# Two hand-kept issue orders of a convolution-and-attention kernel laid anew: the second convolution and the second attention

## The chip, the cores and the metric

The kernel runs on one core of one Trainium2 chip. The time is device microseconds of one execution, and the median of three executions of the kernel before is 421.01 us (420.74 to 422.48). The core has five instruction streams that run on their own and meet at semaphores: TensorE (PE in the profile, with PEld its weight loads), VectorE (DVE), ScalarE (ACT), GpSimd (POOL) and SyncE (SP), which here only issues DMAs. An engine takes its instructions in the order in which the program emitted them; an instruction that waits holds up all that stand behind it on the same engine.

## The reference: what is computed

`x` is `A_u`, 2048 tokens of 512 channels in bf16. Four residual layers are applied, two kinds twice each:

```
x = x + A(layernorm(x))      # convolution, first
x = x + B(layernorm(x))      # attention, first
x = x + A(layernorm(x))      # convolution, second
x = x + B(layernorm(x))      # attention, second
```

`A` is a diagonal state-space layer: a kernel `K[d, l]`, the real part of a sum over 128 poles, is convolved with each channel over all 2048 tokens by FFT (causal, padded to 4096), and `u * Dskip` is added. `B` is a local attention with 32 heads of 16 channels: `qkv = x @ wqkv`; a token looks at 8 keys, itself and those 2, 4, ... 14 tokens back, keys before the first token are masked, softmax over the 8, and the result goes through `wo`.

## The kernel before

**Layout.** Token `16 p + j` lies in partition `p` at index `j` of the residual tile `X` (128 partitions, 16 values of `j`, 512 channels), which stays in the chip's memory from start to end. Channels are handled in four chunks `dc` of 128; `cp` names the half of the channels (chunks 0 and 1, or 2 and 3). In the attention `fp` is a half of the heads and `jh` a half of the `j`.

**How order is set.** Every layer records its steps with `Plan.op`, each with its engine letter and the steps that it needs, and `Plan.either` records several ways to do one step (on another engine, or by DMA). `Plan.run` then emits the steps in the order of a row of numbers, `ORDERS[turn]`: turn 0 is the convolution kernel and the first convolution, turn 1 the first attention, turn 2 the second convolution (`a_layer`), turn 3 the second attention (`b_layer`). A row of numbers so sets two things: the order on every engine, and which of the ways is taken, since only the numbers of that way are in the row. Nothing is planned at run time.

**The second convolution** (`a_layer`), for each chunk `dc`:

- `s1`: PE multiplies the normed `U` by `F1` (L1120), and ACT or DVE copies the sums to `Z` (L1124).
- `turn`: a quarter `c` of `Z` is turned, either by a transposing DMA that SP issues (L1135), or by PE (L1141) with a copy to `zt` by ACT or DVE (L1145).
- `s2`: PE (L1161), and ACT copies to `xc` (L1165).
- `load`: the spectrum of the kernel, tile `Kt`, comes from DRAM scratch. POOL or SP loads it whole in two DMAs of 256 KB (L1224), or SP loads half of it in two of 128 KB (L1229, "once") and DVE copies it to the other partitions (L1234, "other"). The ring holds 8 of these tiles, of 16 in all.
- `product`: DVE multiplies `xc` by `Kt` (L1174).
- `inverse`: PE (L1186), and ACT or DVE copies to `VT` (L1189), as a whole or in two halves.
- `final`: PE adds `X` (L1204, L1207), and ACT or DVE writes `X` (L1212).

**The second attention** (`b_layer`):

- `start`: `X` is turned into `XT` (printed as `U`) by SP's transposing DMAs (L1318) or once by PE (L1312, L1315). DVE gathers the row statistics of a token group, for 512 channels at once into `ln_st` (L200), or for 256 at a time into `pst` (L1370), which can begin when one half of the channels is there; then the aggregates (L204, L1374) and the root on ACT (L1385, L1386).
- `pairs`: the reciprocal deviations `rs` are moved down a partition by PE (L1412) with a copy (L1414), DVE forms the products `rr` (L1417), ACT spreads them to `RR` (L1397), and POOL sets a few entries to one (L1403).
- `pair` and `proj`: PE projects queries and keys (L1450, L1431), and copies follow (L1455, L1436); `ahead` copies the end of the keys to the front (L1473). `values` projects the values (L1485), copied with a scale to `VX` (L1496), and SP moves some of them down a partition (L1509).
- `logits`: DVE multiplies q by k (`prod`, L1530) and PE sums (`Lp`, L1541); a copy, a turn and a copy lay them out as `L` (L1559, L1567, L1572).
- `softmax`: POOL masks (L1617), DVE scales by `RR` (L1610), takes the maximum in three steps (L1591) and subtracts it (L1655, or PE does); ACT takes the exponential, PE sums (`ps_den`, L1647), ACT inverts (L1628, L1632), and DVE multiplies (L1675).
- `pv`: DVE multiplies values by weights (`prod`, L1706) and PE sums into `po`; ACT copies to `ot` (L1748), and SP turns it into `oT` (L1753).
- `out`: PE multiplies by `wo` (L1818), row group `j` by row group. There are four ways to add the residual: PE adds it by an identity matmul and ACT copies (way 0 in the lower row groups); DVE adds from PE's sums (L1793); ACT copies to `sp` (L1797) and DVE adds (L1800); or ACT copies and POOL issues an adding DMA (L1803).
- `stored`: SP or ACT issues the store of a row group (L1967).

```
self.ops.append((fn, flat(after), self.way))
...
order = [int(i) for i in ORDERS[Plan.turn].split()]
...
for i in order:
    fn, after, way = self.ops[i]
    assert done.issuperset(after)
    fn()
```

Of the kernel before, what the change touches and what calls it, by code (L numbers as in the profile page):

```python
# [231 lines left out]
def load_params(nc, pp, prm):  # L232
# [53 lines left out]
    "792 813 936 747 853 854 741 843 789 742 935 938 750 855 937 844 845 748 751 870 939 940 869 821 822 859 752 753 872 "  # L286
    "871 790 829 830 812 873 860 943 942 862 861 924 925 926 910 946 874 911 912 945 948 863 864 947 865 876 867 949 877 "
    "950 953 951",
    "388 127 32 47 4 165 52 128 134 135 141 160 143 146 151 147 6 272 152 155 11 12 170 18 20 23 24 179 184 177 178 358 "
    "28 30 359 68 365 366 192 193 372 373 379 381 194 195 66 67 227 56 228 205 206 197 57 95 216 217 58 96 230 37 198 "  # L290
    "204 248 249 412 413 106 107 407 408 255 256 262 269 270 219 73 264 208 231 74 436 76 399 232 220 394 109 84 437 85 "
    "221 42 209 386 77 215 78 98 110 111 414 87 415 241 242 99 100 439 383 88 92 447 282 448 93 425 426 238 239 120 384 "
    "417 284 121 387 418 419 289 315 316 304 305 117 428 429 299 283 118 337 338 392 393 450 307 294 326 327 275 451 452 "
    "430 308 318 440 441 278 319 320 340 341 329 330 347 310 467 331 458 311 351 352 469 460 348 349 464 465 461 462",
    "34 87 44 1 122 33 178 8 121 149 130 259 151 36 119 63 136 229 9 179 230 231 180 196 120 150 62 64 65 205 125 37 148 "
    "152 50 206 207 197 198 202 35 181 93 203 182 204 260 38 247 183 232 261 274 248 275 233 39 126 40 41 42 153 265 216 "
    "66 386 388 390 391 389 124 392 123 127 393 387 249 234 276 319 128 67 172 223 224 173 394 400 175 320 225 176 325 "
    "326 395 398 399 396 397 401 402 286 287 406 408 412 410 292 293 289 290 310 311 313 314 283 284 404 405 418 407 316 "
    "317 307 308 298 280 299 302 177 419 420 421 422 413 281 409 411 414 343 423 344 334 335 295 296 352 328 353 322 474 "
    "476 323 337 424 338 416 475 417 453 477 480 331 332 304 305 429 430 431 481 478 479 482 375 376 454 438 455 340 341 "  # L300
    "363 484 364 485 355 356 456 507 346 347 457 511 349 508 358 350 486 487 359 509 512 462 463 366 367 460 369 461 370 "
    "360 361 488 384 441 489 372 378 373 379 385 439 440 490 493 495 494 381 496 445 497 498 499 442 382 443 444 446 447 "
    "506 449 450 452 464 465 521 519 466 523 520 524 522 525 526 473 527 513 514 510 533 530 534 537 529 515 517 518 547 "
    "532 804 805 806 832 833 784 785 535 822 767 548 823 824 549 550 536 551 552 553 768 786 558 559 538 560 539 540 794 "
    "839 567 568 580 541 569 576 581 544 808 795 578 543 577 579 582 572 852 583 546 574 573 575 570 840 571 584 587 599 "
    "588 600 853 601 602 591 592 810 595 597 939 855 586 598 589 593 706 596 590 702 594 603 841 921 925 926 694 922 708 "
    "796 695 703 709 707 927 696 697 883 923 834 873 924 704 698 968 699 884 908 813 857 700 705 701 874 906 863 710 864 "
    "940 811 859 953 954 854 941 955 971 969 893 904 894 862 909 974",
]


# [1691 lines left out]
```

## Time and profile before

| what | value |
|---|---|
| median of 3 executions | 421.01 us |
| profiled execution, its own time | 421.17 us |
| span of the profiled execution | 419.4 us, 13672 instructions |
| DVE busy | 393.0 us, 94% |
| PE busy | 355.7 us, 85% |
| ACT busy | 326.4 us, 78% |
| POOL busy | 29.1 us, 7% |
| second convolution | from about 268 to 308 us of the span |
| second attention | from about 308 us to the end |

Busy time is the sum of an engine's instructions, and neighbours on DVE and ACT overlap by some hundredths of a microsecond, so a group's mean is a little more than what one more of its kind adds. The view by windows gives the busy time of each engine within a stretch and the granted PE clock; where an engine is busy for nearly the whole stretch, it sets the pace there. The timeline gives in brackets the idle time ahead of a group and the releaser. SP's DMA rows show the issue, and the landing comes later.

### The profile page before, as it was taken

Reading aid. Unit: us, or ns where it says so; the run is one execution under the profiler, and the core shown is the slowest. Engines: PE = TensorE matmul, PEld = TensorE weight load, DVE = VectorE, ACT = ScalarE, POOL = GpSimd, SP = SyncE. Lnnn points to the kernel's source line nnn. Section 1 sums busy time; section 2 is a strip of 40 time slices with the busy share of each in tenths; the row PEclk is TensorE's granted clock in tenths of the full one; section 3 lists DMA queues with packets and bytes.
Section 4 is the critical chain, followed back from the end, with each engine's and each line's share of the span. In section 5 each row is a group of like instructions: output and inputs, shape, how many; then the busy total and the mean of one; then the engine's idle time right before and its main releaser. Section 6 shows DMA issues by size and latency. Waiting matters only on the chain. (4 is left out here: it accounts for less than half of the span.)

```text
span 419.4 us, 13672 instructions
## 1 busy us (share of the span) xinstructions
PE 355.7 (85%) x5866; PEld 226.9 (54%) x5866; DVE 393.0 (94%) x652; ACT 326.4 (78%) x534; POOL 29.1 (7%) x99
## 2 busy tenths in 40 slices
PE   2268867987998989999975999899999999966995
PEld 1153645776786764446732444677874456632452
DVE  6999999999999887989999999999999999999994
ACT  7999999899999574678963599999966788762730
POOL 2000000000000200010100303020000010000331
PEclk9999999999999999999999899999999999995899
DMA  7997248697989666002336277899972000352496
GB/s 212 214 294 265 95 57 166 151 163 176 167 129 167 135 166 125 19 2 70 89 98 91 54 151 140 167 182 199 202 87 57 19 2 2 88 134 56 52 174 143
DMA packets 103538, 52.01 MB, mean 124 GB/s; under 512 B 82923, under 2 KB 95356, under 8 KB 103222
## 3 DMA queue, kind: packets, MB, share of 16 engines
q1 hardware_dynamic: 97638, 44.46, 51.6%
q0 software_dynamic: 3376, 5.37, 6.8%
q10 hardware_dynamic: 2464, 1.31, 1.1%
q8 instruction: 46, 0.75, 0.8%
q14 instruction: 14, 0.11, 0.1%
HBM read 19.30 MB, written 6.29 MB: 61 GB/s over the span
## 5 line engine op out<-in xcount | busy, mean ns | idle before, releaser
L1706 DVE TENSOR_TENSOR prod<-VX,L 128x512 bf16<-128x512 bf16 (+2 forms) x72 | 75.5, 1102 | 0.5 <-ACT VX L1496 0.2
L1530 DVE TENSOR_TENSOR prod<-qT,kT 128x4096 bf16<-128x4096 bf16 (+1 forms) x40 | 72.3, 1857 | 0.5 <-ACT kT L1436 0.3
L1818 PE MATMUL ps_o<-wo_t,oT 128*32 128x512 bf16 x512 | 33.9, 395 | 0.4 <-DMA oT<-ot 0.4
L1485 PE MATMUL ps_v<-wv,U 128*128 128x256 bf16 x256 | 31.6, 272 | 1.7 <-ACT VX L1496 1.0
L877 ACT CAST Z<-ps_s 128x1024 bf16<-128x1024 f32 (+1 forms) x36 | 31.9, 931 | 0.5 <-PE ps_s L874 0.4
L1431 PE MATMUL ps_qk<-U,wqk 128*128 128x512 bf16 x128 | 30.3, 380 | 0.7 <-ACT qT L1436 0.7
L1496 ACT ACTIVATE VX<-ps_v,rs 128x256 bf16<-128x256 f32 x64 | 26.8, 472 | 3.8 <-PE ps_v L1485 3.0
L1485 PEld LDWEIGHTS <-U 128*128 128x128 bf16 x256 | 24.5, 97 | 9.6 <-issue 5.1
L1450 PE MATMUL ps_qk<-U,wqk 128*128 128x512 bf16 x128 | 28.8, 379 | 0.8 <-ACT X L1212 0.8
L1541 PE MATMUL Lp<-prod,sb_bones 128*32 128x512 bf16 x256 | 22.3, 409 | 5.6 <-DVE prod L1530 5.6
L1748 ACT CAST ot<-po 128x1024 bf16<-128x1024 f32 (+1 forms) x15 | 14.4, 985 | 14.2 <-PE po L1721 10.5
L1721 PE MATMUL po<-prod,sb_ident 32*32 32x512 bf16 x768 | 17.1, 428 | 7.5 <-DVE prod L1706 7.3
L894 PE MATMUL xp<-zt,sb_C 128*128 128x512 bf16 x64 | 18.9, 379 | 4.2 <-ACT zt L914 2.3
L1818 PEld LDWEIGHTS <-oT 128*32 128x32 bf16 x512 | 13.1, 99 | 14.7 <-issue 3.5
L1431 PEld LDWEIGHTS <-wqk 128*128 128x128 bf16 x128 | 11.8, 98 | 17.0 <-issue 4.8
L1450 PEld LDWEIGHTS <-wqk 128*128 128x128 bf16 x128 | 12.4, 98 | 15.2 <-issue 1.1
L969 DVE TENSOR_TENSOR pa<-sp_u,sp_k 128x2048 bf16<-128x2048 bf16 x16 | 19.4, 1221 | 0.8 <-ACT sp_k L905 0.5
L874 PE MATMUL ps_s<-KT,FK 128*128 128x128 bf16 (+1 forms) x360 | 18.8, 209 | 1.0 <-ACT KT L847 0.5
L1174 DVE TENSOR_TENSOR pa<-xc,Kt 128x2048 bf16<-128x2048 bf16 x16 | 18.9, 1221 | 0.6 <-PE vp L1186 0.3
L874 PEld LDWEIGHTS <-FK 128*128 128x128 bf16 x360 | 17.4, 98 | 3.2 <-issue 2.3
L983 PE MATMUL vp<-sb_IC,pa 128*128 128x128 bf16 x256 | 17.0, 219 | 1.7 <-DVE pa L969 0.8
L905 ACT CAST sp_k<-xp 128x1024 bf16<-128x1024 f32 x16 | 16.5, 1046 | 1.8 <-PE xp L894 1.5
(234 smaller groups left out, 862.3 us busy)
## 6 DMA issues: line engine op xcount, KB each, us to landing
kt_scratch<-sp_k SPq DMA_DIRECT2D x16, 256.0 KB, 2.8
Kt<-kt_scratch POOLq DMA_DIRECT2D x16, 256.0 KB, 6.1
sp_u<-sp_u SPq DMA_DIRECT2D x18, 128.0 KB, 3.5
X<-in_A_u_dram SPq DMA_DIRECT2D x8, 256.0 KB, 5.3
X<-in_A_u_dram SPq DMA_DIRECT2D x4, 512.0 KB, 5.6
Kt<-kt_scratch SPq DMA_DIRECT2D x8, 256.0 KB, 5.3
VX<-VX SPq DMA_DIRECT2D x4, 448.0 KB, 3.7
VX<-VX SPq DMA_DIRECT2D x4, 336.0 KB, 3.3
```

What stands on the lines that cost most here:

```text
L874: nc.tensor.matmul(ps[:, r, 0:n // 4, jj * 4:(jj + 1) * 4], w, x, start=(k == 0), stop=(k == len(todo) - 1))
L877: nc.scalar.copy(box["Z", kind, dc, b0][:, 0:n // 4, :, jq * 16:(jq + 1) * 16].rearrange("p g r k -> p r g k"), box.pop(("s1", kind, dc, j ...
L894: nc.tensor.matmul(xp[:, h, :], C2[:], z[:, 4 * h:4 * h + 4, :], start=True, stop=True)
L969: nc.vector.tensor_tensor(pr[:], box["U"][:, s:t + 1:t - s], k[:].unsqueeze(1).to_broadcast([128, 2, 1024]), ALU.mult)
L1431: nc.tensor.matmul(ps[:], wqk[:, ct, f0:f0 + 128], XT[:, ct // 2, 4 * s:4 * s + 4, ct % 2, :], start=(ct == 0), stop=(ct == 3))
L1450: nc.tensor.matmul(box[name][:, k * 512:k * 512 + 512], wqk[:, ct, f0:f0 + 128], XT[:, ct // 2, 4 * s:4 * s + 4, ct % 2, :], start=(ct == ...
L1485: nc.tensor.matmul(ps[:, jj].rearrange("p t h d -> p (t h d)"), XT[:, ct // 2, j + jj, ct % 2, :], wv[:, ct, fp * 256:(fp + 1) * 256], sta ...
L1496: nc.scalar.activation(out, ps, ACT.Identity, scale=r)
L1530: nc.vector.tensor_tensor(pr[:], windows(q, 0, 2), windows(kT[fp][:, a:a + n2, col(w):col(w) + 1024], -DIL * 128, 2), ALU.mult)
L1541: nc.tensor.matmul(Lp[r0:r0 + 32, w // 4, :], bones[:, w % 4 + k, :], pr[:, k, f2 - a, hb * 512:(hb + 1) * 512], start=(n == 1 and k == 0) ...
L1706: nc.vector.tensor_tensor(p2[:].rearrange("p w j t d h -> p w (j t) d h"), windows(v, -DIL * 256, taps), l.to_broadcast([128, taps, nj * 2 ...
L1818: nc.tensor.matmul(ps[r:r + 32], lhsT, rhs, start=(ft == -1 or ft == 0 and not res), stop=(ft == 3), skip_group_check=True)
```

## The change

Only two rows of the table are replaced: `ORDERS[2]` and `ORDERS[3]`. All functions, tiles and pool sizes stay. The lines begin:

```
-    "388 127 32 47 4 165 52 128 134 135 141 160 143 146 151 147 6 272 152 155 11 12 170 18 20 23 24 179 184 177 178 358 "
...
+    "43 32 47 165 281 52 160 155 4 127 134 128 141 146 135 151 147 143 152 6 11 12 179 184 18 20 358 359 177 178 23 365 "
...
-    "34 87 44 1 122 33 178 8 121 149 130 259 151 36 119 63 136 229 9 179 230 231 180 196 120 150 62 64 65 205 125 37 148 "
...
+    "35 78 77 44 1 167 33 87 162 79 8 38 39 34 196 178 81 229 9 230 231 107 36 166 169 179 105 180 130 259 136 205 168 "
```

**Which ways change, in the second convolution.** Two quarters of `Z`, (chunk 0, quarter 0) and (3, 2), that PE turned and DVE copied are now turned by SP's DMA: 10 DMA turns become 12, and 6 turns on PE become 4. Of the copies of `Z`, DVE takes one more of 128x1024 and one fewer of 128x512, ACT the reverse. DVE's copies to `VT` go from three whole ones and two halves to three and four, ACT's from eleven and two to nine and four. Both copies of 128x4x128 to `X` go from DVE to ACT. One whole `Kt` tile, (0, 2), is loaded by SP instead of POOL; four half loads with DVE copies stay four, for other tiles.

SP in the second convolution, one piece of the difference. `Kt` is the spectrum, `zt` a turned quarter of `Z`; L1229 are the half loads.

```order
 L1135 DMA_TRANSPOSE zt<-Z 128x8x128 x6
+L1229 DMA Kt<-kt_scratch 64x1024 x2
+L1135 DMA_TRANSPOSE zt<-Z 128x8x128 x4
+L1224 DMA Kt<-kt_scratch 64x2x1024 x2
 L1229 DMA Kt<-kt_scratch 64x1024 x6
-L1135 DMA_TRANSPOSE zt<-Z 128x8x128 x3
-L1229 DMA Kt<-kt_scratch 64x1024 x2
 L1135 DMA_TRANSPOSE zt<-Z 128x8x128
-L1224 DMA Kt<-kt_scratch 64x2x1024 x4
+L1224 DMA Kt<-kt_scratch 64x2x1024 x2
+L1135 DMA_TRANSPOSE zt<-Z 128x8x128
+L1224 DMA Kt<-kt_scratch 64x2x1024 x2
```

Before, six half loads stood right behind the sixth turn. Now a half load of two DMAs, four turns and a whole load stand there first, and the six half loads (tiles (3,0), (3,1) and (2,1)) come after them. The last half loads and turns are interleaved anew.

**Which ways change, in the second attention.** Row statistics: the groups 1 and 3 now go by halves of the channels and group 2 by 512, so that there are 24 half gathers and 4 whole ones instead of 16 and 8. DVE instead of ACT makes the copies of `rs` (L1414), of one key block (L1436) and of the end of the keys of (fp 1, f2 1) (L1473; SP now does that of f2 0). Residual sums: row group 0 no longer uses the identity matmul; DVE's sums from PE go from 7 to 5, its sums from `sp` from 1 to 5, POOL's adding DMAs from 7 to 6. Stores: SP issues 11 instead of 8, ACT 5 instead of 8.

ACT around the spread of `RR` (L1397), before and now. `kT` and `qT` are keys and queries, `L` the logits as the softmax takes them.

```order
L1414 COPY rs<-ps_down 128x14
L1436 CAST kT_6721<-ps_qk 128x512
L1455 CAST qT_6722<-ps_qk 128x1024
L1397 CAST RR<-rr 128x512 x2
L1436 CAST kT_6721<-ps_qk 128x512
L1559 CAST LT<-Lp 128x1024
L1436 CAST kT_6721<-ps_qk 128x512 x2
L1436 CAST qT_6723<-ps_qk 128x512 x2
L1436 CAST kT_6721<-ps_qk 128x512
L1436 CAST qT_6723<-ps_qk 128x512
L1572 COPY L_6724<-pt_l 128x512 x2
```

```order
L1559 CAST LT<-Lp 128x1024
L1436 CAST kT_6705<-ps_qk 128x512 x2
L1436 CAST qT_6707<-ps_qk 128x512 x2
L1436 CAST kT_6705<-ps_qk 128x512
L1436 CAST qT_6707<-ps_qk 128x512
L1572 COPY L_6708<-pt_l 128x512 x2
L1397 CAST RR<-rr 128x512 x2
```

The spread has moved from ahead of the first `LT` copy to behind the first copies to `L`. On POOL the setting of `RR` to one (L1403) has moved from behind the first mask (L1617) to ahead of it.

DVE at the end of the kernel, before and now. L1706 are the last products with the values, L1793 and L1800 residual sums, L1750 the last copy to `oT`.

```order
L1706 TENSOR_TENSOR prod_8258<-VX,L_6725 128x512
L1793 TENSOR_TENSOR X<-ps_o,X 128x2x256
L1706 TENSOR_TENSOR prod_8279<-VX,L_6725 128x512
L1706 TENSOR_TENSOR prod_8323<-VX,L_6725 128x512
L1706 TENSOR_TENSOR prod_8325<-VX,L_6725 128x512
L1793 TENSOR_TENSOR X<-ps_o,X 128x2x256
L1706 TENSOR_TENSOR prod_8336<-VX,L_6725 128x512
L1793 TENSOR_TENSOR X<-ps_o,X 128x2x256
L1750 CAST oT<-po 128x512
L1793 TENSOR_TENSOR X<-ps_o,X 128x2x256 x4
```

```order
L1706 TENSOR_TENSOR prod_8257<-VX,L_6709 128x512
L1793 TENSOR_TENSOR X<-ps_o,X 128x2x256
L1706 TENSOR_TENSOR prod_8274<-VX,L_6709 128x512
L1800 TENSOR_TENSOR X<-sp,X 128x2x256
L1750 CAST oT<-po 128x512
L1800 TENSOR_TENSOR X<-sp,X 128x2x256 x2
L1793 TENSOR_TENSOR X<-ps_o,X 128x2x256 x2
L1800 TENSOR_TENSOR X<-sp,X 128x2x256
L1793 TENSOR_TENSOR X<-ps_o,X 128x2x256 x2
```

Before, residual sums stood between the last five products; now all but the last product are ahead of the first sum from PE, and three of the late sums take `sp`, which ACT has copied. The last sum is that of row group 8 instead of 11, and its store goes by ACT instead of SP.

36 rows, old and new, of the table ORDERS are left out of this document.

## The prediction

> **What bounds the kernel now.** I read the page first, for the shares, then the busy times in nine stretches from the start of the second convolution, since a share of the whole span says nothing of the two layers that change.
>
> ```profile
> 267.90:287.00 19.10, 18.05 (x246) 14.74 (x246) 18.48 (x21) 18.65 (x22) 2.38 (x4) 1.00 0.99 171
> 287.00:308.00 21.00, 20.82 (x294) 17.35 (x292) 19.82 (x25) 19.92 (x23) 0.00 (x0) 1.00 1.10 184
> ...
> 320.00:340.00 20.00, 20.00 (x120) 8.80 (x119) 19.43 (x23) 14.39 (x29) 1.47 (x16) 1.00 0.05 20
> 340.00:362.00 22.00, 21.34 (x205) 13.18 (x203) 20.45 (x19) 18.43 (x37) 1.45 (x13) 1.00 0.09 25
> 362.00:381.00 19.00, 13.17 (x294) 8.39 (x293) 18.64 (x13) 10.11 (x22) 0.00 (x0) 0.88 0.39 98
> ...
> 405.00:419.40 14.40, 9.15 (x157) 4.61 (x154) 8.15 (x17) 1.17 (x2) 2.41 (x2) 0.93 0.69 157
> ```
>
> Behind the length of each stretch stand the busy times of PE, PEld, DVE, ACT and POOL, then the granted clock, the DMA share and GB/s. In the convolution (the first two rows) PE, DVE and ACT are each busy for 94% or more and the DMA engines are full too, so work cannot be shifted there without a price. From 320 to 362 us PE has next to nothing free and DVE little. From 362 to 381 DVE alone is full (18.64 of 19.00, PE 13.17). The last stretch is PE's again, 9.15 us of it from 405 to its last product at 414.2.
>
> The chain of work that ended last tells what the final stretch hangs on (start, length, what):
>
> ```profile
> 386.55 1.08 PE po L1721 x32
> ...
> 414.20 0.69 DVE X L1793
> ```
>
> From 386.5 us on it runs over PE's sums and output products, up to one DVE sum. That sum ends at 414.20 + 0.69 = 414.89; the remaining 419.4 - 414.89 = 4.51 us are the last stores.
> The profiled execution took 421.17 us, its span 419.4; the median of three is 421.01, so 0.16 us are taken off at the end. Gains or losses under 0.5%, 2.1 us, count as no change: that is about what a measurement of this kernel can tell from none.
>
> **The convolution.** The durations, as groups by form (busy, mean ns, idle before):
>
> ```profile
> L1124 DVE CAST Z<-ps_s 128x1024 bf16<-128x1024 f32 x5 | 6.0, 1221 | 0.4 <-PE ps_s L1120 0.4
> L1145 DVE COPY zt<-pt 128x1024 bf16<-128x1024 bf16 x6 | 4.1, 686 | 0.2
> L1189 DVE CAST VT<-vp 128x1024 bf16<-128x1024 f32 x3 | 3.7, 1222 | 0.2 <-PE vp L1186 0.2
> L1189 DVE CAST VT<-vp 128x512 bf16<-128x512 f32 x2 | 1.4, 692 | 0.2 <-PE vp L1186 0.2
> L1212 DVE CAST X<-ps_y 128x512 bf16<-128x512 f32 x2 | 1.3, 681 | 0.0
> 270.45 0.61 PE L1141 MATMUL pt<-sb_ident,Z 128*128 128x128 bf16 x8
> ```
>
> DVE, up to the last product: one `Z` copy of 1.221 for one of 128x512 (the 0.681 of L1212, same shape and source), two `zt` copies of 0.686 fewer, and for `VT` one whole and four halves where two wholes and one half stood: +0.540 - 1.372 + (3.990 - 3.136) = +0.02 us, nothing. Behind the last product it loses 0.83 us (two copies to `X` and a half, for one whole), at a place where PE is the fuller engine (20.82 of 21.00), so I count it at zero. PE loses two turns of eight products, 2 x 0.61 = 1.22 us; where PE idles (1.05 us before 287) this moves the idle only, and I count zero, with a gain up to the idle time of DVE, 0.62 + 1.18 = 1.80 us, as the lower end.
>
> What can cost is the queue of SP, which now has two more turns and holds six of the half loads behind four turns and a whole load.
>
> ```profile
> 269.88 11.15 SPq L1135 DMA_TRANSPOSE zt<-Z  x6
> 282.22 4.63 SPq L1229 DMA_DIRECT2D Kt<-kt_scratch  x6
> 291.98 1.15 SPq L1229 DMA_DIRECT2D Kt<-kt_scratch  x2
> 294.71 3.26 SPq L1224 DMA_DIRECT2D Kt<-kt_scratch  x4
> L1135 SPq DMA_TRANSPOSE zt<-Z x10: 1232/1252/2061, 269.9 to 293.2; - x10
> DMA to landing us min/median/max: 3.2/4.2/6.6
> DMA to landing us min/median/max: 4.4/4.7/4.9
> 292.16 0.88 DVE L1234 COPY Kt<-Kt 64x1024 bf16<-64x1024 bf16 x2
> ```
>
> (The first landing row is of the turns, the second of the half loads.) Six turns took 11.15 us, 1.86 each, though one issues in 1.25: SP waits for quarters of `Z`. They end at 281.03. Now the first six hold a quarter that is ready early, so they may end one pace sooner, at 279.2. Behind them stand a half load (1.15), four turns at 1.25 (5.0) and a whole load (half of 3.26, 1.63): the half loads of tile (3,0) start at 287.0 to 288.8 instead of 282.22. Its second DMA goes 4.63/6 = 0.77 later and lands 4.7 after that, at 292.5 to 294.3. DVE copied from it at 292.16 and found it there. So it is now 0.3 to 2.1 us late, 1.2 in the middle. DVE has 1.18 us of idle time in this stretch (19.82 of 21.00), half of which can be used up by a wait that comes earlier: I take **+0.6 us**. The upper end is four turns at the pace of 1.86: 2.4 us later than 288.8, landing at 296.7, or 4.5 us late. The ends are -1.8 and +4.5.
>
> On the landing the Trainium skill has a rule (DMA: Bandwidth & Descriptors, section "Anatomy of one DMA — SWDGE (gpsimd) path"): about 2.0 us of fixed cost and the bytes at 436 GB/s, stated for DMAs that GpSimd issues. My estimate by that page for a half load's 128 KB is 2.3 us, with no wait at DVE, a term of zero and a time of 420.5 us; the 4.4 to 4.9 of the row were measured with the DMA engines full, and I go by the row.
>
> **The attention, up to the weights.** DVE has eight half gathers more and four whole ones fewer, a copy of the key ends, a key copy from PE's sums (nearest row: the 0.681 of L1212 above, same shape) and the small copy of `rs` (nearest: an aggregate of 0.157).
>
> ```profile
> L1370 DVE BATCH_NORM_STATS2 pst<-X 128x6 f32<-128x256 bf16 x16 | 5.8, 410 | 0.0
> L200 DVE BATCH_NORM_STATS2 ln_st_a<-X 128x6 f32<-128x512 bf16 x8 | 5.1, 681 | 0.6 <-ACT X L1212 0.6
> L1473 DVE COPY kT<-kT 128x768 bf16<-128x768 bf16 x1 | 0.4, 363 | 0.8 <-ACT kT L1455 0.8
> L204 DVE BATCH_NORM_AGGREGATE ln_mv_a<-ln_st_a 128x2 f32<-128x6 f32 x8 | 0.8, 157 | 0.0
> ```
>
> That is 8 x 0.410 - 4 x 0.681 + 0.363 + 0.681 + 0.157 = 1.76 us more. What it meets is this place:
>
> ```profile
> 328.21 11.39 DVE L1530 TENSOR_TENSOR prod<-qT,kT 128x2048 bf16<-128x2048 bf16 x6
> 330.14 1.14 ACT L1397 CAST RR<-rr 128x512 bf16<-128x512 f32 x2
> 337.70 1.08 ACT L1572 COPY L<-pt_l 128x512 bf16<-128x512 bf16 x2
> 339.43 0.76 POOL L1403 MEMSET RR<- 1x16 bf16 x10
> 340.15 0.69 DVE L1610 TENSOR_TENSOR L<-L,RR 128x1024 bf16<-128x1024 bf16 x1 [0.55 <-POOL RR L1403]
> 353.35 0.69 DVE L1675 TENSOR_TENSOR L<-L,sm_rdb 128x1024 bf16<-128x1024 bf16 x1 [0.97 <-ACT sm_rdb L1632]
> ```
>
> The products end at 328.21 + 11.39 = 339.60 and DVE then waits for `RR`. Now the spread follows the copy to `L`: 338.78 + 1.14 = 339.92, and POOL's setting makes 340.7, or 0.5 later than before. Queued behind the spread on ACT are query and key copies, for which PE and the next `prod` wait. But DVE's own products end 1.76 later, at 341.4, so `RR` is there, and the sum with `RR` begins 341.4 - 340.15 = 1.2 us late. Behind it DVE has the wait of 0.97 us, which can take most of that up, and at the start PE's wait of 0.75 us may shrink, where a turn of `X` by PE now stands ahead of the second projections:
>
> ```profile
> 311.83 0.59 PE L1450 MATMUL ps_qk<-U,wqk 128*128 128x512 bf16 x2 [0.75 <-ACT X L1212]
> ```
>
> I take **+0.3 us**: 1.2 - 0.97 = 0.2, and a tenth put on for the spread. The ends are -0.75 (that PE wait gone, all else hidden) and +2.9 (nothing hidden: 1.76 + 1.14).
>
> **The tail.** PE no longer multiplies four identities for row group 0:
>
> ```profile
> 262.19 0.39 PE L1818 MATMUL ps_o<-X,sb_ident 128*32 128x512 bf16 x4
> L1793 DVE TENSOR_TENSOR X<-ps_o,X 128x512 bf16<-128x512 f32 x7 | 4.7, 690 | 1.7 <-PE ps_o L1818 1.7
> L1800 DVE TENSOR_TENSOR X<-sp,X 128x512 bf16<-128x512 bf16 x1 | 0.4, 418 | 0.0
> 411.26 3.93 ACTq L1967 DMA_DIRECT2D out_dram<-X  x6
> DMA to landing us min/median/max: 1.9/3.4/4.1
> DMA to landing us min/median/max: 3.2/3.7/4.7
> ```
>
> (The first landing row is of the stores, the second of POOL's adding DMAs.) By duration four identities are worth 0.39 us, a little less where neighbours overlap; on a chain that is PE throughout, this comes off: -0.3. DVE's residual sums cost 4 x 0.418 - 2 x 0.690 = +0.29, in a stretch where its waits for `ps_o` come to 1.7 us, hence nothing. Before, six stores of ACT stood in one row from 411.26 to 415.19, and from the last sum to the end went 4.51 us. An issue (3.93/6 = 0.66) and a median landing make 4.06. With five stores on ACT and earlier sums the last ones should be less bunched, worth about 0.5. Term **-0.8 us**; ends -2.3 (0.39, and 1.95 if the last store lands in the least 1.9) and +1.0 (the turn of the last `ot` on SP now stands behind two stores that wait for adding DMAs; landing at 4.7 instead of 3.7).
>
> **Sum.** 421.17 + 0.6 + 0.3 - 0.8 = 421.27, less 0.16: **421.1 us**.
>
> **Rivals.**
>
> *SP falls behind (slower).* The point that decides is whether the four turns ahead of the half loads issue at 1.25 or at the 1.86 of the first six. At 1.86 DVE waits 4.5 us at its copy of tile (3,0), all products and inverses behind it too: 421.17 + 4.5 + 0.3 - 0.8 - 0.16 = 425.0. For it: the pace of the row, and a landing of up to 6.6. Against it: most of that pace is the wait for quarters of `Z`, and with two turns less PE makes these a little earlier. Chance 0.20.
>
> *DVE's and ACT's lateness is not taken up (slower).* If `sm_rdb`, itself made from DVE's results, moves along with them, the 0.97 stays a wait, and 1.76 + 1.14 = 2.9 us are on the path: 421.17 + 0.6 + 2.9 - 0.8 - 0.16 = 423.7. For it: PE and DVE are both nearly full from 320 to 362. Against: the wait of 0.97 starts when DVE is done, whatever it had to do before. Chance 0.14.
>
> *The idle time goes (faster).* Half of DVE's idle in the convolution (0.9), PE's 0.75 at 311.83 and half of the tail's lower end (1.2): 421.17 - 2.85 - 0.16 = 418.2. For it: less PE work in the two stretches where PE is full. Against: the idle is scattered in waits of under 1 us. Chance 0.28.
>
> **How the numbers follow.** My own forecast has 0.38. Faster by over 0.5% (under 418.9): 0.28; slower (over 423.1): 0.20 + 0.14 = 0.34; within: 0.38. The likeliest single case gives 421.1, its own range 418.9 to 423.1. The range goes from 417.3 (the faster rival with all of DVE's idle, another 0.9) to 426.8 (SP behind, with the tail's upper end: 425.0 + 1.8).
>
> **What would show it.** Right: the copy of tile (3,0) on DVE shows a wait of about 1 us on a DMA; the sum with `RR` begins about 1 us later within the attention, with no wait for POOL; the wait for `sm_rdb` is gone; PE's last product ends some 0.3 us sooner relative to the start of the tail, and less than 4.5 us lie between the last sum and the end. Wrong: `Kt` waits on DVE of over 3 us, turns with landings above 5 us for which PE waits, a new wait of PE or DVE over 1 us between 340 and 362, or a last store that waits for an adding DMA of POOL.

## The result: 0.8 percent slower, in two places

The changed kernel takes 425.11 us (median of 6 executions, 424.97 to 426.76), the kernel before 421.93 us (median of 6, 420.74 to 422.84). The ratio is 1.0084, with a 95% interval from 1.0061 to 1.0107. That is outside the likeliest case (418.9 to 423.1) and inside the range (417.3 to 426.8).

The profiled execution of the changed kernel is its slowest, 426.76 us with a span of 425.0; the other five took 424.97 to 425.19. Some of that lies in layers that the change does not touch. The rows are PE's busy time and clock from 20 to 40 us, first before, then after (length, PE, PEld, DVE, ACT, POOL, clock, DMA share, GB/s):

```profile
20.00:40.00 20.00, 14.57 (x349) 9.34 (x350) 19.75 (x68) 19.94 (x32) 0.00 (x0) 1.00 0.89 262
```

```profile
20.00:40.00 20.00, 14.77 (x346) 9.26 (x347) 19.94 (x69) 19.94 (x32) 0.00 (x0) 0.59 0.87 268
```

The granted clock was 0.59 there, and the second convolution starts 1.19 us later (DVE's first copy to `Z` at 269.06 instead of 267.87). All kernels of this document are alike up to that copy: in the four traces without such a stretch it begins at 267.5 to 267.9, in the seven with one at 268.1 to 269.8. So I measure all traces from that copy. All times of this table are microseconds behind it, each worked out from rows of DVE's timeline and the span:

| point | before | after | later by |
|---|---|---|---|
| last product of the convolution ends | 36.79 | 39.02 | 2.23 |
| first sum with `RR` (L1610) begins | 72.28 | 75.80 | 3.52 |
| last multiplication of the weights (L1675) begins | 128.03 | 130.47 | 2.44 |
| last residual sum ends | 147.02 | 152.84 | 5.82 |
| end of the span | 151.53 | 155.94 | 4.41 |

By stage: the convolution lost 2.2 us, the attention up to the weights 0.2, the tail up to the last sum 3.4, and 1.4 came back behind that sum. The 4.41 us are those of two single executions; the ratio of 1.0084 is about 3.5 us.

**The convolution.** DVE's and PE's waits (total, times, longest), DVE's row at the half load, SP's rows, the issue times of the turns in ns (shortest, median, longest), and the landings of turns and of half loads:

```profile
DVE Kt L1234 <- DMA Kt<-kt_scratch: 2.6, 1, 2.6
PE xp L1161 <- DMA zt<-Z: 1.6, 2, 1.3
296.21 1.95 DVE L1234 COPY Kt<-Kt 64x1024 bf16<-64x1024 bf16 x4 [2.62 <-DMA Kt<-kt_scratch]
271.08 9.94 SPq L1135 DMA_TRANSPOSE zt<-Z  x6
282.42 8.34 SPq L1135 DMA_TRANSPOSE zt<-Z  x4
290.86 1.26 SPq L1224 DMA_DIRECT2D Kt<-kt_scratch  x2
292.29 3.67 SPq L1229 DMA_DIRECT2D Kt<-kt_scratch  x6
L1135 SPq DMA_TRANSPOSE zt<-Z x12: 1231/1253/3390, 271.1 to 299.4; - x12
DMA to landing us min/median/max: 3.1/4.6/7.0
DMA to landing us min/median/max: 3.4/3.9/5.9
```

The copy of tile (3,0) waits 2.62 us for its half load, which SP issues at 292.29 behind four turns that took 8.34 us, 2.1 each. They did not wait for `Z`: ACT's last copy to it ran from 282.48 to 283.55, the second of the four turns was issued at 283.77, and all four follow each other with gaps of 0.4 us in all. The issues themselves were long, 1.25, 3.39, 1.23 and 2.10 us, where the longest of before took 2.06. PE now waits for turns too.

**The attention up to the weights.** DVE at its start, at the first sum with `RR` and at the first weights:

```profile
312.97 2.73 DVE L1370 BATCH_NORM_STATS2 pst<-X 128x6 f32<-128x256 bf16 x8 [1.63 <-ACT X L1212]
336.06 8.89 DVE L1530 TENSOR_TENSOR prod<-qT,kT 128x4096 bf16<-128x4096 bf16 x4
344.86 0.69 DVE L1610 TENSOR_TENSOR L<-L,RR 128x1024 bf16<-128x1024 bf16 x1
357.69 0.69 DVE L1675 TENSOR_TENSOR L<-L,sm_rdb 128x1024 bf16<-128x1024 bf16 x1
```

The last three rows have no wait in brackets any more. The first has a longer one than any of before at that place (0.36 us), for a copy to `X` by ACT. The sum with `RR` is 3.52 - 2.23 = 1.3 us later against the convolution's end, and 1.1 of that has gone by the last weights (2.44).

**The tail.** First before: SP's first six turns of `ot`, their landings, POOL's adding DMAs around the sixth, and PE's first products of row group 12. Then the changed kernel: the same turns and adding DMAs, the chain of waits (start, length, what), and PE's timeline:

```profile
373.80 26.18 SPq L1753 DMA_TRANSPOSE oT<-ot  x6
DMA to landing us min/median/max: 3.2/3.3/3.4
399.04 2.41 POOL L1803 DMA_DIRECT2D X<-sp  x2 [2.73 <-ACT sp L1797]
403.63 0.61 PE L1818 MATMUL ps_o<-wo_t,oT 128*32 128x512 bf16 x8
```

```profile
378.40 26.49 SPq L1753 DMA_TRANSPOSE oT<-ot  x6
400.75 2.40 POOL L1803 DMA_DIRECT2D X<-sp  x2 [2.66 <-ACT sp L1797]
402.42 0.47 ACT sp L1797
402.89 5.53 DMA oT<-ot
...
421.21 0.69 DVE X L1793
406.11 0.39 PE L1818 MATMUL ps_o<-wo_t,oT 128*32 128x512 bf16 x2
408.47 0.94 PE L1818 MATMUL ps_o<-wo_t,oT 128*32 128x512 bf16 x6 [1.96 <-DMA oT<-ot]
409.34 2.31 PE L1735 MATMUL po<-sb_ident,prod 128*128 128x128 bf16 x20
412.33 1.31 PE L1735 MATMUL po<-sb_ident,prod 128*128 128x128 bf16 x20
```

PE comes to the output products of row group 12 and waits 1.96 us for the sixth turn of `ot`, which landed 5.53 us after its issue at 402.89, where before it took 3.4. Before, two adding DMAs were issued just behind that turn (from 399.04, the turn at 398.7); now they are issued 2.1 us ahead of it. Then 20 sums take 2.31 us where 20 later ones take 1.31. The windows show the clock lower there (the column after POOL's):

```profile
408.40:409.40 1.00, 0.93 (x7) 0.18 (x8) 0.00 (x0) 0.00 (x0) 0.00 (x0) 0.60 1.09 154
409.40:411.60 2.20, 2.20 (x26) 2.00 (x24) 1.61 (x4) 0.00 (x0) 0.00 (x0) 0.50 1.27 169
413.00:415.00 2.00, 2.00 (x37) 1.02 (x34) 1.86 (x6) 0.57 (x1) 0.00 (x0) 1.00 0.26 75
```

Behind the last sum it is shorter than before, 425.0 - 421.90 = 3.10 us instead of 4.51. The stores issued after 413 us before (first row) and after 417 us now land like this:

```profile
DMA to landing us min/median/max: 3.1/4.0/4.1
DMA to landing us min/median/max: 1.8/1.9/2.3
```

### The profile page after: what moved, and what is told of

It reads as the page before. It is cut to its first block, busy times and chain, and to the rows that moved or that the text cites. A ratio compares the mean times of both kernels' runs of the same rounds, so it can differ in the third digit from the quotient of the medians.

```text
span 425.0 us, 13638 instructions
## 1 busy us (share of the span) xinstructions
PE 358.2 (84%) x5846; PEld 227.4 (54%) x5846; DVE 393.6 (93%) x659; ACT 326.7 (77%) x535; POOL 26.8 (6%) x96
## 5 line engine op out<-in xcount | busy, mean ns | idle before, releaser
L1706 DVE TENSOR_TENSOR prod<-VX,L 128x512 bf16<-128x512 bf16 (+2 forms) x72 | 75.6, 1103 | 4.1 <-PE po L1735 3.6
L1165 ACT CAST xc<-xp 128x1024 bf16<-128x1024 f32 x16 | 16.0, 1047 | 2.6 <-PE xp L1161 2.6
```

Source lines behind the costliest of these rows:

```text
L1706: nc.vector.tensor_tensor(p2[:].rearrange("p w j t d h -> p w (j t) d h"), windows(v, -DIL * 256, taps), l.to_broadcast([128, taps, nj * 2 ...
```

## The experiments

Theory 1: two places in the queues make the loss, SP's turns in the convolution, and the last turns of `ot`. Theory 2: the extra work of DVE and the moved spread of `RR` make it. Each run was timed beside the kernel before on the same chip. The numbers in the edits are steps of the two rows.

**conv_only and attn_only.** One new row each.

```diff
 conv_only:  ORDERS[2] new, ORDERS[3] of before
 attn_only:  ORDERS[2] of before, ORDERS[3] new
```

> Only the new order of the second convolution; the second attention keeps the order of before. Theory 1 (two waits make the loss: DVE's 2.62 us for the half load of tile (3,0), and PE's 1.96 us for the last turns of ot, with PE at half clock behind it): the wait for Kt is there again, 2 to 3 us, and the time is 1.8 to 2.4 us above before. Theory 2 (the loss is the extra DVE work and the moved spread of RR in the attention, the convolution hides its wait): within 0.5 us of before.

> Only the new order of the second attention; the convolution keeps the order of before. Theory 1: 0.3 us lost up to the weights, 3.3 us in the tail by PE's wait for oT and its slow clock, 1.4 us won back behind the last sum: 1.5 to 2.5 us above before, with PE's wait for oT in the trace again. Theory 2: all of the loss, 3 to 4 us above before, and the lateness stands at the first sum with RR already.

Measured: 1.0040 (1.0020 to 1.0059) and 1.0040 (1.0022 to 1.0059), so about 1.7 us each, and together 0.80 of the 0.84%. The attention alone has its last weights 0.19 us later than before (128.22 instead of 128.03 behind the first copy to `Z`), its last sum 3.54 later and its end 2.61 later, in an execution that is the slowest of its twelve (424.84, median 423.65). Theory 2 falls: the convolution does not hide its wait, and the attention is hardly late at its weights. The waits of the new attention, then those of the new convolution:

```profile
PE ps_o L1818 <- DMA oT<-ot: 2.0, 1, 2.0
DVE prod L1706 <- PE po L1735: 3.6, 2, 3.2
```

```profile
PE xp L1161 <- DMA zt<-Z: 2.8, 1, 2.8
DVE VT L1189 <- PE vp L1186: 3.0, 1, 3.0
DVE Kt L1234 <- DMA Kt<-kt_scratch: 1.3, 1, 1.3
```

In this execution (424.14, median 423.13) the new convolution loses 3.5 us, and the larger part at PE, for a turn, not at DVE for the half load, whose wait of 1.3 us is below the 2 to 3 that I expected. So "the half load is late" was not the whole of it.

**kt_early.** SP around the moved half loads:

```diff
-L1135 DMA_TRANSPOSE zt<-Z 128x8x128 x4
+L1135 DMA_TRANSPOSE zt<-Z 128x8x128 x2
+L1229 DMA Kt<-kt_scratch 64x1024 x4
+L1135 DMA_TRANSPOSE zt<-Z 128x8x128 x2
 L1224 DMA Kt<-kt_scratch 64x2x1024 x2
-L1229 DMA Kt<-kt_scratch 64x1024 x6
+L1229 DMA Kt<-kt_scratch 64x1024 x2
```

> The changed kernel, with the half loads of tiles (3,0) and (3,1) put on SP two turns earlier. Theory 1: DVE's wait for Kt falls from 2.62 to under 0.5 us, and the time is about 2 us below the changed kernel (423.0 against 425.1). Rival (SP has no room: what is put ahead makes the turns late): PE waits for zt instead, 1.5 us or more, and the time stays within 0.7 us of the changed kernel.

Measured: 1.0076 (1.0048 to 1.0104), no gain. The rows are DVE's largest wait in the convolution, and POOL's load of tile (0,1):

```profile
291.20 1.23 DVE L1174 TENSOR_TENSOR pa<-xc,Kt 128x2048 bf16<-128x2048 bf16 x1 [2.30 <-DMA Kt<-kt_scratch]
L1224 POOL DMA_DIRECT2D Kt<-kt_scratch x2: 601/604/606, 284.6 to 285.2; - x2
```

The wait of 2.3 us has gone to the product of tile (0,1). Its load by POOL now starts at 284.6, where the changed kernel's started at 279.9: the half loads, recorded ahead of it, took the buffer that it used to get. So the run did not test the place on SP by itself. The next one does.

**kt_early2.** The same with that load (37) ahead:

```diff
-... 270 284 ...
+... 270 37 383 386 284 ...
```

> The changed kernel with the half loads of (3,0) and (3,1) two turns earlier on SP, and POOL's load of tile (0,1) recorded ahead of them, so that it keeps its place among the eight buffers. Theory 1 (their place on SP makes them late): no wait for Kt over 0.5 us, the last product of the convolution 1.5 to 2.3 us earlier than in the changed kernel. Rival (SP's turns and the DMA engines have no slack, each piece put ahead makes another late): PE waits for a turn of zt, or DVE for another tile, 1.5 us or more, and the last product ends within 0.7 us of the changed kernel's.

Measured: 1.0076 (1.0041 to 1.0111). The last product ends at 40.93, later than the changed kernel's 39.02:

```profile
DVE Kt L1234 <- DMA Kt<-kt_scratch: 3.6, 1, 3.6
PE xp L1161 <- DMA zt<-Z: 3.2, 2, 2.4
```

The copies of (3,0) and (3,1) wait no more, but the half load of (2,1), which stayed behind the turns, is waited for 3.6 us, and PE waits 3.2 us for turns. The rival holds: SP's queue has no room there, and what is put ahead makes another piece late.

**turns_on_pe.** The two turns back on PE and DVE (53 and 404 are the DMA turns):

```diff
-... 66 53 394 ... 204 404 269 ...
+... 66 56 57 394 ... 204 407 408 269 ...
```

> The changed kernel with the two quarters of Z, (0,0) and (3,2), turned by PE and copied by DVE again as before, so that SP has 10 turns instead of 12; all else as changed. Theory 1 (the two turns on SP's queue make the half loads late): the half loads of tile (3,0) are issued about 3 us earlier, DVE's wait for Kt falls under 0.7 us, and the last product of the convolution ends 1 to 2 us earlier; time 1 to 2 us below the changed kernel. Rival (the place of the half loads behind four turns does it, or the 2.6 us of work given back to PE and DVE cost as much): the last product ends within 0.5 us of the changed kernel's.

Measured: 1.0051 (1.0029 to 1.0073). The last product ends at 37.16, 1.86 us earlier than in the changed kernel and within 0.4 of before. DVE's only wait in the convolution of 0.2 us or more, and SP's rows:

```profile
DVE Z L1124 <- PE ps_s L1120: 0.4, 2, 0.2
281.22 5.62 SPq L1135 DMA_TRANSPOSE zt<-Z  x3
288.74 3.68 SPq L1229 DMA_DIRECT2D Kt<-kt_scratch  x6
```

The six half loads stand behind the turns here as well, but are issued at 288.74. The three turns ahead of them were issued in 1.23 to 1.35 us each. With two turns fewer no one waits for SP. So in the traces 1.86 of the 2.23 us go with these two turns, and the place of the half loads alone costs nothing. The times say it less sharply: the intervals of 1.0051 and 1.0084 overlap.

**outs_later.** PE's first products of row groups 12 and 14 (911, 939) behind the last sums of piece 12:

```diff
-... 599 911 593 ... 589 939 591 ... 590 592 694 ...
+... 590 592 911 939 694 ...
```

> The changed kernel, with the first halves of the output products of row groups 12 and 14 moved on PE behind the last sums of piece 12, so that the turn of ot has about 1.3 us more to land. Theory 1: PE's wait of 1.96 us goes, the stretch at half clock behind it goes too, DVE's wait of 3.0 us for po goes, and the time is 2.5 to 3.5 us below the changed kernel. Rival (the wait only changes its place, since the products of DVE or the turn's landing of 5.5 us set the pace there): under 1 us below, with a wait of PE for prod or for oT of over 1 us.

Measured: 1.0078 (1.0052 to 1.0103), no gain, though DVE's last product with the values ends at 142.83, as before (142.58). PE's timeline, the chain, and the clock behind the wait:

```profile
413.27 6.20 PE L1818 MATMUL ps_o<-wo_t,oT 128*32 128x512 bf16 x80 [1.89 <-DMA oT<-ot]
406.49 6.73 DMA oT<-ot
414.00:416.00 2.00, 2.00 (x28) 0.81 (x24) 1.10 (x2) 0.56 (x1) 0.00 (x0) 0.52 0.47 138
```

The first wait is gone, and the next turn is late: the last `ot`, which SP issues behind the stores of row groups 5 and 6, and which took 6.73 us to land. The rival holds: the wait has changed its place. Theory 1 had two late turns, but I had expected the one to free the other.

**tail_mended and stores_behind.** Old convolution; the first has both moves, the second only that of the stores (857, 859):

```diff
-... 573 857 576 ... 584 859 586 599 ...
+... 584 586 857 859 599 ...
```

> The convolution of before with the new attention, its tail changed in two places: on PE the first halves of the output products of row groups 12 and 14 stand behind the last sums of piece 12, and on SP the stores of row groups 5 and 6 stand behind the last turn of ot instead of ahead of it. Theory 1 (the tail's loss is the two late turns, each by its place: one reached too early by PE, one queued behind stores that wait for adding DMAs): neither wait of PE for oT is over 0.5 us, no stretch at half clock behind 400 us, the last sum ends 3 to 4 us earlier than with the new attention as it is, and the time is 0.5 to 1.5 us below before. Rival (the landing of the turns is long because the DMA engines are full there, wherever the turns stand): PE still waits over 1 us for oT and the time stays 1 to 2 us above before.

> The convolution of before, the new attention, and of the two moves in the tail only the one on SP: the stores of row groups 5 and 6 behind the last turn of ot. Theory 1 (PE reaches the products of row group 12 before the sixth turn has landed, whatever SP does): PE's first wait for oT of about 2 us and the half clock behind it stay, and the time is as with the whole new attention, 1.2 to 2 us above before. Rival (those two stores hold up the sixth turn's landing as well): the wait falls under 1 us and the time to within 0.5 us of before.

Measured: tail_mended 0.9977 (0.9959 to 0.9995), faster than before by 0.2%; stores_behind 1.0046 (1.0027 to 1.0065). PE's waits from 390 us on, its last row and SP's rows in the first, then PE's wait in the second:

```profile
PE po L1735 <- DVE prod L1706: 0.2, 1, 0.2
409.73 4.94 PE L1818 MATMUL ps_o<-wo_t,oT 128*32 128x512 bf16 x88
374.98 30.10 SPq L1753 DMA_TRANSPOSE oT<-ot  x7
405.18 10.48 SPq L1967 DMA_DIRECT2D out_dram<-X  x11
```

```profile
PE ps_o L1818 <- DMA oT<-ot: 2.0, 1, 2.0
```

Only both moves together take the waits away. Behind the first copy to `Z` the last sum then ends at 147.91 instead of 150.56, 2.65 us earlier where I expected 3 to 4. The sixth and seventh turn still land late there, 5.6 and 5.5 us after their issue; PE now comes later than that. The interval of tail_mended lies just under 1, and its 0.2% is small beside the spread of single executions (420.32 to 422.90).

**both_mended.** The changed kernel with turns_on_pe and both moves of the tail.

> The changed kernel with both repairs: quarters (0,0) and (3,2) turned by PE again, and the two moves in the tail. Theory 1 (SP's two turns in the convolution and the two late turns of ot are the whole loss): the time is within 1 us of before, or 3 to 4.5 us below the changed kernel; no wait for Kt or oT over 0.5 us. Rival (something else of the 0.84 percent is left, such as the extra work of DVE): still 1.5 us or more above before.

Measured: 1.0015 (1.0000 to 1.0030), where the changed kernel had 1.0084. With two turns back on PE and four steps of the tail moved, 0.7 of the 0.8% are gone. What is left, about 0.6 us, is at the edge of what these runs tell. But tail_mended, the same tail with the convolution of before, had 0.9977 (0.9959 to 0.9995), and the two intervals do not meet: by the times the new convolution still costs about 0.4% with its two turns back on PE, though its last product ends only 0.32 us later than before in the trace (37.11). Where the rest lies is not shown.

## Why the prediction was right and wrong

The three terms, in us, measured by the table above:

| term | predicted | ends | measured |
|---|---|---|---|
| convolution | +0.6 | -1.8 to +4.5 | +2.2 (3.5 in conv_only) |
| attention up to the weights | +0.3 | -0.75 to +2.9 | +0.2 |
| tail | -0.8 | -2.3 to +1.0 | +3.4 - 1.4 = +2.0 |
| sum | +0.1 | | +4.4 |

**Attention: right in its steps.** The sum with `RR` was to be 1.2 us late and was 1.3, DVE no longer waited for POOL there, the wait for `sm_rdb` was gone, and the lateness went into the idle time. In the changed kernel the 1.3 is partly chance: DVE had 0.83 us less to do behind the convolution's last product, which the forecast counted at zero, and waited 1.63 us at the start for ACT's copy to `X`, which no term had. attn_only, with the convolution of before, is the cleaner check: 73.54 instead of 72.28, 1.26 late. PE's wait of 0.75 us at its start did not shrink.

**Convolution: the mechanism right, its size not.** SP's queue and DVE's copy of tile (3,0) were the place. The step that was mis-sized is "four turns at 1.25": they took 8.34 us, 2.1 each, even slower than the 1.86 that the rival took from the page's own pace. With that the half loads started at 292.29, or 291.1 behind the shift of 1.19, and not at 287.0 to 288.8. I took the usual issue time, 1.25, as the price of each, although the row of before had an issue of 2.06; one of the four took 3.39 and one 2.10. The reason that both the forecast and the rival gave for a slower pace, the wait for quarters of `Z`, was not it, since `Z` was complete before the second of the four. What held these issues up is not shown; with two turns fewer they were short. The half of the wait that I let DVE's idle time pay was not paid either: DVE waited 2.62 and lost 2.2. And I counted the two turns only by what stands behind them; PE's waits for `zt` itself (1.6 us, 2.8 in conv_only) were in no term, though turns that land after more than 5 us and make PE wait stood among the signs of being wrong; the longest landing was 7.0.

The estimate by the Trainium skill (DMA: Bandwidth & Descriptors, section "Anatomy of one DMA — SWDGE (gpsimd) path"), 2.3 us for a half load, is not borne out for these loads, which SP issues: in the changed kernel the shortest landing was 3.4 and the longest 5.9. The row of before (4.4 to 4.9) was the better price.

**Tail: the sign was wrong, and +2.0 lies outside the ends of the term.** Both gains that I counted came: the identities went, and the stores landed sooner (1.4 us against 0.5 expected). The step that failed is the one that called the chain "PE throughout" and priced only what PE does. I did not follow PE's new order against the turns: in the row of before the sixth turn was issued by 398.7 and PE used it from 403.63 on, 4.9 us later; now it was issued at 402.9 and PE was there at 406.5, after 3.6. The new margin alone would not have cost anything: the turn had landed in 3.4 before. It cost 1.96 us since the landing took 5.5 as well. In five other traces with the new attention the turn is issued 2.1 us behind the adding DMAs too and lands in 5.6; in before and conv_only, with the old attention, it is issued at about the time of the first of them and lands in 3.4 and 4.3. So PE's order and the longer landing made the wait together; that the adding DMAs lengthen the landing was not tried. The risk that I did name, the last turn behind two stores, is real (outs_later shows it) but was hidden here by the first wait, and its price of +1.0 was too small: 1.89 us of wait, and the clock on top.

**The rivals.** SP falling behind gave 425.0, and 425.1 was measured; that is partly chance, since the convolution had only 2.2 of the 4.5 us of that rival and the tail gave the rest. That the time lies inside the range is chance in the same way: the convolution's upper end made the room that the tail, beyond its own, took up. DVE's lateness was taken up; the idle time did not go.

## What to carry to other kernels

Price a transfer that is moved to a full queue by the longest issues in its row as well as by the usual one, and ask who waits for the transfer itself as well as for what stands behind it. Where the order of a consumer changes, work out for each transfer how long after its issue the consumer comes, and compare that with the longest landing of such a transfer anywhere in the profile. The turns of `ot` alone showed at most 3.4 us before, but the turns of `Z`, among full DMA engines, 6.6. When one late transfer is mended, look for the next: here either move in the tail was worth nothing that could be measured alone, and both together took the ratio from 1.0040 to 0.9977.

## What was not expected of the hardware

A short wait of PE was in several traces followed by a stretch at about half of the granted clock, which cost more on top of it: in the changed kernel 6 products took 0.94 us, and 20 sums 2.31 instead of 1.31. After 1.96 us the clock was 0.60 and 0.50 for some 3 us; after 1.89 it was 0.52 (outs_later); in conv_only, after 2.76 us:

```profile
288.00:289.00 1.00, 0.61 (x1) 0.28 (x3) 0.97 (x2) 0.00 (x0) 0.00 (x0) 0.50 2.32 83
289.00:290.00 1.00, 0.97 (x3) 0.42 (x3) 0.80 (x2) 0.73 (x1) 0.00 (x0) 0.50 0.42 85
```

It is no fixed rule, and that the wait is the cause is not shown: in stores_behind a wait of 2.00 us at the same place left the clock at 1.00, where I had expected the half clock again.

```profile
408.00:410.00 2.00, 2.00 (x36) 1.45 (x33) 1.98 (x6) 0.00 (x0) 0.00 (x0) 1.00 1.28 96
```

The Trainium skill (TensorE: Matmul & The Clock Gate, section "Part 1: The HAM clock gate") gives half rate as the state after at least one idle window of about 3.4 us. The rate agrees; the waits here were shorter than that window, so why some of them were enough stays open.

The landing of one kind of DMA also spreads widely: turns of `ot` of one size took 3.2 to 6.7 us within outs_later, the longest issued right behind two stores of SP. Which transfers hold the others up was not tried.
